# Attention's probabilities turned in one VectorE instruction per unit, the values product in 32x64 tiles, and PSUM cut into three pairs of banks and two single ones

## The chip, the cores and the metric

The kernel runs on one core of a Trainium2 chip. The metric is the device time of one execution in microseconds (us). Before the change it is 827.86 us, the median of three runs (825.67 to 829.38). The engines are named as in the profile: PE is TensorE's matmul, PEld its weight load, DVE is VectorE, ACT is ScalarE, POOL is GpSimd, SP is SyncE, which issues every DMA of this kernel.

## The reference

Attention with two kinds of windows, and two MLPs on its output, all in float32:

```
q, k, v: [4 batches, 8 heads, 576 positions, 64]
scores = q @ k.T / 8
allowed: rel = query - key;  heads 0 to 3: 0 <= rel < 32
                             heads 4 to 7: 0 <= rel < 128 and rel % 4 == 0
attn = exp(scores - max);  attn = attn / (sum(attn) + 1e-9);  out = attn @ v
x = out as [2304 tokens, 512]
x = g(x @ w_in) @ w_out,    g(h) = h / (1 + exp(-1.702 h)),   512 -> 2048 -> 512
x = r(x @ w_in2) @ w_out2,  r(h) = max(h, 0)**2,              512 -> 2048 -> 512
```

## The kernel before, in words

**Attention.** The positions of heads 4 to 7 are reordered by their remainder modulo 4, so that both kinds of heads have a window of 32. The work is cut into 32 *units*: four batches, four pairs of heads (`p`; the two heads of a pair, `j`, lie on the two halves of the partitions) and two halves of the positions (`u`). A unit has 288 queries in three blocks of 96, and each block sees 128 keys. A unit (`attend`) runs through these steps: two loads by SP (`qk`, L476, and `v`, L480); scores on PE (L514); per head and block a maximum with the mask added on DVE (L530) and an exponential with its sum on ACT (L538); `guard` and `recip` (L552, L555) and the division (`normalise`, L562); the turning of the probabilities so that keys lie on partitions; the values product on PE (L616); and two copies into `x`, a rounded high part (L271 on ACT or L273 on DVE) and the rest (L632 on DVE).

There are two ways to score and to turn. In batch 0 (`turn_pe`) a block of 96 queries is scored against its 128 keys by one matmul per head, with masks of 96x128, and turned by PE against an identity (L597), with a copy of the result out of PSUM for each head (`evac`, 128x288). In batches 1 to 3 only the band is computed: per block three groups of 32 queries against their 64 keys, 18 small matmuls in tiles of 64 rows by 32 columns, and the turning takes six DVE instructions of 32x192 (L582) into a tile `pt` that is zero elsewhere. In both the values product is six matmuls of 128 rows by 64 columns, 96 moving columns each.

**Layer 1.** The 2304 tokens are worked in five blocks of 512, 512, 256, 512 and 512 (`BLOCKS1`). In a block, 16 steps (`step`, index `f`) each take 12 matmuls into a bank `h` (L664 to L666), a tanh on ACT (L688), a product on DVE (L691), a split into `gh` and `gl`, and 12 matmuls into four banks `o` (L716 to L718). Every product in full precision is three matmuls of rounded parts, high times high, high times low, low times high. The weights of layer 1 are loaded (`raw`, L332), reassembled by `raw_top` (`c`, L271) and `raw_join` (L343), and split into `wp` high and low while block 0 runs. Batch 0's units come ahead of block 0; the other 24 units are strewn between the matmuls of blocks 0 to 2, eight to each.

**Layer 2** uses seven products for eight, in three pieces of 768 tokens, with weights streamed in from DRAM where blocks 3 and 4 had stored them.

**What sets the order.** All of it is written down as tasks with an engine (or a choice of ACT, DVE, POOL), a cost, a wanted time and buffers. `Schedule.run` takes them one by one in the order of their modelled starts, and emits each engine's instructions in that order. The costs, the wanted times and the margins at the head of the file decide the order, and the chip keeps it. In gaps of PE that the model foresees ahead of layer 1 it emits matmuls on zeros (L775).

**PSUM** has eight banks. Before, four are `o` (layer 1's outputs; early on also scores and values of batch 0), two are `h`, two are `s` (scores, and the values of batches 1 to 3).

Of the kernel before, what the change touches and what calls it, by code (L numbers as in the profile page):

```python
# [37 lines left out]
T_START = 29.61  # L38
T_ATT = 2.78
A0 = 0.27  # L40
A1 = 0.99
BAND_FROM = 1

AHEAD = (32, 35, 48)
# [6 lines left out]
PREP = 9.48  # L51
# [3 lines left out]
RAW_FROM = 3.07  # L55
WARM = 256
MASK_AT = -9.0
LEAD = (12.09, 8.0, 5.51)
SPACE = 3.94
# [3 lines left out]
SPARE_POOL = (3.96, 1.14, 0.0)  # L63
SPARE_ACT = (0.0, 0.07, 0.01)
SPARE_TO = (7.79, 224.45)
# [26 lines left out]
X_EARLY = 18.11  # L92
X_FROM = 2.03
X_WANT = 6.23


class Schedule:
# [3 lines left out]
    def __init__(self, places):  # L101
        self.sizes = places
        self.tasks = []
        self.idle = None

    def buffer(self, cls):
        return {"cls": cls, "users": 0}

    def task(self, engine, cost, want, fn, after=(), bufs=(), port=False, since=0.0, late=0.0):
# [4 lines left out]
            "since": since, "late": late, "n": len(self.tasks), "next": [], "before": 0, "worse": 0.0,  # L114
# [11 lines left out]

    def open(self, t):
        for e, cost in t["ways"].items():
            ready = max([end + (self.SAME[e] if d == e else self.HOP[d] + MORE_HOP) for end, d in t["ready"]] + [t["since"]])
            self.opened[e].append((t, ready, cost, t["worse"] if e == "dve" else 0.0))  # L130

    def run(self, emit):

        engines = self.SAME
        places = {c: [(0.0, None)] * n for c, n in self.sizes.items()}
# [11 lines left out]
        for _ in range(len(self.tasks)):  # L147
# [34 lines left out]
            for b in t["bufs"]:  # L182
                if not b["held"]:
                    b["held"] = True
                    by = places[b["cls"]].pop(0)[1]
# [7 lines left out]
            t["engine"], t["start"] = e, start  # L193
            self.order.append(t)
            if e == "dma":
                issued = max(start, issued) + 0.45
# [7 lines left out]
            for b in t["bufs"]:  # L204
# [3 lines left out]
                if b["left"] == 0:  # L208
                    c = places[b["cls"]]
                    c.append((b["end"] + self.HOP[e], b["by"]))  # L210
                    c.sort(key=lambda p: p[0])
# [9 lines left out]
def attention_mlp_mlp(  # L221
# [18 lines left out]
    psum = {  # L240
        "o": ctx.enter_context(tc.tile_pool(name="ps_o", bufs=4, space=PSUM)),
        "h": ctx.enter_context(tc.tile_pool(name="ps_h", bufs=2, space=PSUM)),
        "s": ctx.enter_context(tc.tile_pool(name="ps_s", bufs=2, space=PSUM)),
    }
# [8 lines left out]
    ident = att.tile([QB, QB], F32, name="ident")  # L253
    mask_sb = att.tile([QB, 5, P], BF16, name="mask_sb")
    mask_band = att.tile([QB, 5, 2 * WIN], BF16, name="mask_band")
    pt = att.tile([P, 2, NBLK, QB], F32, name="pt")

    places = {
        "o": 4, "h": 2, "s": 2, "c": C_BUFS, "qk": 2, "v": 2, "sm": 2, "st": 3, "pt": 1,
# [4 lines left out]
    sched = Schedule(places)  # L264
    task, buffer = sched.task, sched.buffer
# [31 lines left out]
    def bank(cls, name):  # L297
        return psum[cls].tile([P, 512], F32, tag=cls, name=name)
# [105 lines left out]
    def x_pieces(b, p, u):  # L404

        plain = p < NPAIR // 2
        m = HALF // 4
        jobs = []
        for n, blk in enumerate(BLOCKS1):
            size = sum(e - a for _, _, a, e in blk)  # L410
            found = []
            col = 0
            for bb, r, a, e in blk:
                if bb == b:
                    if plain:
                        lo, hi = max(a, m * u), min(e, m * (u + 1))
                        if lo < hi:
                            found.append((r, lo, hi, col + lo - a))
                    elif r // 2 == u:
                        found.append(((r % 2) * ROW + a, (r % 2) * ROW + e, col))  # L420
                col += e - a
            if plain:
                while found:
                    r, lo, hi, c = found.pop(0)
                    rows = 1
                    while (
                        found
                        and found[0] == (r + rows, lo, hi, c + rows * ROW)
                        and c >= lo % ROW
                        and c - lo % ROW + (rows + 1) * ROW <= size  # L430
                    ):
                        found.pop(0)
                        rows += 1

                    def src(o, r=r, rows=rows, lo=lo, hi=hi):
                        v = o[:, 0:HALF].rearrange("p (i r) -> p r i", r=4)
                        v = v[:, r:r + rows, lo - m * u:hi - m * u]
                        return v if rows > 1 else v[:, 0]

                    def dst(x, z, c=c, rows=rows, lo=lo, hi=hi):  # L440
                        if rows == 1:
                            return x[:, z, p, c:c + hi - lo]
                        c0 = c - lo % ROW
                        v = x[:, z, p, c0:c0 + rows * ROW].rearrange("p (r i) -> p r i", r=rows)
                        return v[:, :, lo:hi]

                    jobs.append((n, rows * (hi - lo), src, dst))
            elif found:
                s0, c0 = found[0][0], found[0][2]
                w = sum(f[1] - f[0] for f in found)  # L450
                jobs.append(
                    (
                        n, w, lambda o, s0=s0, w=w: o[:, s0:s0 + w],
                        lambda x, z, c0=c0, w=w: x[:, z, p, c0:c0 + w],
                    )
                )
        return jobs

    MAXIMA, EXPS = {P: 0.205, 2 * WIN: 0.145}, {P: 0.385, 2 * WIN: 0.34}
# [948 lines left out]
```

## Time and profile before

| what | value |
|---|---|
| median of three runs | 827.86 us (825.67 to 829.38) |
| the profiled execution | 826.51 us, span 824.5 us |
| granted TensorE clock, mean | 0.998 |
| stretch 0 to 40 us: PE, DVE, ACT, POOL busy | 30.66, 29.70, 31.65, 18.02 us |
| stretch 40 to 150 us: PE, DVE, ACT busy | 109.83, 97.27, 78.99 us |
| stretch 150 to 300 us: PE, DVE, ACT busy | 150.00, 104.59, 71.87 us |
| stretch 300 to 460 us: PE, DVE, ACT busy | 160.00, 128.14, 78.80 us |
| stretch 460 to 821 us: PE, DVE, ACT busy | 361.00, 235.75, 169.80 us |

The span runs from the first to the last instruction; the execution's own time is 2.0 us longer. The first stretch is batch 0's attention, the second most of block 0 (with the weights' preparation), the third blocks 1 and 2, the fourth blocks 3 and 4, the last layer 2. A matmul's busy time is counted to its modelled end and neighbours overlap, so that 100% of PE says that it never stood empty, not that every matmul ran at its peak.

### The profile page before, as it was taken

How to read it: one execution, taken by the hardware profiler on the slowest of the kernel's cores; microseconds unless marked ns; L12 is line 12 of the kernel's file. 1: busy time of each engine (PE TensorE's matmuls, PEld its weight loads, DVE VectorE, ACT ScalarE, POOL GpSimd, SP SyncE). 2: the span in 40 equal slices, each digit the busy share in tenths (PEclk: the TensorE clock that was granted, in tenths of full speed). 3: DMA queues.
4: the chain of work that ended last, by engine and by line, in shares of the span. 5: the costliest groups of instructions: out<-in, count | busy, mean ns of one | idle time of the engine just before them, and what ended most of it. 6: DMA issues, size and time to landing. Idle time of an engine off the chain costs nothing.

```text
span 824.5 us, 14514 instructions
## 1 busy us (share of the span) xinstructions
PE 811.7 (98%) x5412; PEld 729.6 (88%) x5412; DVE 596.0 (72%) x1467; ACT 431.1 (52%) x1061; POOL 18.6 (2%) x28
## 2 busy tenths in 40 slices
PE   7899999999999999999999999999999999999998
PEld 5687777877789988888888899999999999999998
DVE  6898997755568886878697745589545689365784
ACT  6976775544545563445455345435355446355432
POOL 4400000000000000000000000000000000000000
PEclk9999999999999999999999999999999999999999
DMA  7645564211132129988976761697877686767751
GB/s 238 231 150 212 183 207 155 66 50 34 43 101 73 55 87 297 295 290 304 339 265 241 282 239 49 258 331 257 305 276 258 240 342 236 268 249 269 276 208 57
DMA packets 54917, 171.43 MB, mean 208 GB/s; under 512 B 4736, under 2 KB 26944, under 8 KB 49472
## 3 DMA queue, kind: packets, MB, share of 16 engines
q1 hardware_dynamic: 54848, 170.52, 58.8%
q8 instruction: 42, 0.69, 0.3%
q14 instruction: 27, 0.22, 0.1%
HBM read 131.70 MB, written 38.80 MB: 207 GB/s over the span
## 4 chain that ended last, share of the span: by engine, by line
PE 96%; DMA 2%; ACT 1%; DVE 1%; SPq 0%; issue 0%; DVEq 0%
PE o L716 9%; PE h L664 8%; PE o L718 8%; PE o L717 8%; PE h L665 8%; PE h L666 8%; PE X L1097 4%; PE X L1096 4%; PE X L1095 4%; PE X L1252 3%; PE X L1250 3%; PE X L1251 3%; PE pv L616 2%; PE Y L1252 2%; PE Z L1097 2%; PE Y L1250 2%
## 5 line engine op out<-in xcount | busy, mean ns | idle before, releaser
L664 PE MATMUL h<-x,wp 128*128 128x512 f32 (+3 forms) x328 | 122.1, 372 | 0.2 <-DVE g L691 0.2
L716 PE MATMUL o<-gh,wp 128*128 128x512 f32 (+3 forms) x328 | 122.2, 372 | 0.0
L665 PE MATMUL h<-x,wp 128*128 128x512 f32 (+3 forms) x328 | 119.5, 364 | 0.4 <-DVE x L632 0.3
L666 PE MATMUL h<-x,wp 128*128 128x512 f32 (+3 forms) x328 | 119.3, 364 | 0.0
L717 PE MATMUL o<-gh,wp 128*128 128x512 f32 (+3 forms) x328 | 119.3, 364 | 0.0
L718 PE MATMUL o<-gl,wp 128*128 128x512 f32 (+3 forms) x328 | 119.3, 364 | 0.0
L271 ACT CAST gh<-gq 128x768 fp32r<-128x768 f32 x84 | 68.9, 837 | 74.4 <-PE X L1251 20.9
L282 DVE TENSOR_TENSOR gl<-gq,gh 128x768 fp32r<-128x768 f32 x84 | 80.4, 957 | 28.1 <-PE X L1252 12.2
L688 ACT ACTIVATE g<-h 128x512 f32<-128x512 f32 (+3 forms) x82 | 44.6, 545 | 82.7 <-PE h L666 82.6
L716 PEld LDWEIGHTS o<-gh,wp 128*128 128x128 f32 x328 | 61.7, 188 | 12.0
L664 PEld LDWEIGHTS h<-x,wp 128*128 128x128 f32 x328 | 61.8, 188 | 11.9 <-DVE g L691 0.3
L691 DVE SCALAR_TENSOR_TENSOR g<-g,h 128x512 f32<-128x512 f32 (+3 forms) x82 | 50.8, 620 | 29.2 <-ACT g L688 28.3
L718 PEld LDWEIGHTS o<-gl,wp 128*128 128x128 f32 x328 | 61.8, 188 | 10.0
L665 PEld LDWEIGHTS h<-x,wp 128*128 128x128 f32 x328 | 61.8, 188 | 10.0 <-DVE x L632 0.8
L666 PEld LDWEIGHTS h<-x,wp 128*128 128x128 f32 x328 | 61.8, 188 | 10.0
L717 PEld LDWEIGHTS o<-gh,wp 128*128 128x128 f32 x328 | 61.8, 189 | 9.5
L538 ACT ACTIVATE sm<-sm,st 96x64 f32<-96x64 f32 (+1 forms) x180 | 62.4, 349 | 13.8 <-DVE st L530 13.6
L582 DVE STREAM_TRANSPOSE pt<-sm 32x192 f32<-32x192 f32 x144 | 53.1, 368 | 5.8 <-ACT sm L277 3.8
L282 DVE TENSOR_TENSOR gl<-g,gh 128x512 fp32r<-128x512 f32 (+3 forms) x82 | 51.0, 622 | 7.3 <-ACT gh L271 6.1
L1117 DVE TENSOR_TENSOR gq<-u,Z 128x384 f32<-128x384 f32 x48 | 26.6, 554 | 40.6 <-ACT u L271 23.8
L271 ACT CAST gh<-g 128x512 fp32r<-128x512 f32 (+3 forms) x56 | 33.7, 601 | 37.2 <-DVE g L691 18.6
L271 ACT CAST c<-raw 128x512 f16<-128x512 bf16 x52 | 40.5, 779 | 22.6 <-DMA raw<-in_w 21.5
(131 smaller groups left out, 1796.5 us busy)
## 6 DMA issues: line engine op xcount, KB each, us to landing
ws<-wo_s SPq DMA_DIRECT2D x42, 1024.0 KB, 7.1
raw<-in_w SPq DMA_DIRECT2D x64, 511.8 KB, 4.9
ws<-wi_s SPq DMA_DIRECT2D x36, 896.0 KB, 6.4
wo_s<-wt SPq DMA_DIRECT2D x16, 896.0 KB, 6.9
wi_s<-wt SPq DMA_DIRECT2D x16, 896.0 KB, 6.5
qk<-in_qkv SPq DMA_DIRECT2D x32, 304.0 KB, 2.9
v<-in_qkv SPq DMA_DIRECT2D x32, 192.0 KB, 2.3
xs<-x2d SPq DMA_DIRECT2D x12, 384.0 KB, 4.8
```

The source lines that it names most:

```text
L271: A.copy(out, in_)
L282: by_name[e].tensor_tensor(out=out, in0=a, in1=b, op=ALU.subtract)
L538: A.activation(out=m["sm", j][:, i], in_=m["sm", j][:, i], func=AF.Exp, bias=m["st"][:, 0, j, i:i + 1], scale=-1.0, accum_out=m["st"][:, 1 ...
L582: V.transpose(out=pt[32 * e:32 * e + 32, :, :, 32 * a:32 * a + 32].rearrange("p j i q -> p (j i) q"), in_=m["sm"][32 * a:32 * a + 32, :, : ...
L664: T.matmul(out, w_hi[:, ks], x[:, 0, k, a:z], start=(k == 0), stop=False)
L665: T.matmul(out, w_hi[:, ks], x[:, 1, k, a:z], start=False, stop=False)
L666: T.matmul(out, w_lo[:, ks], x[:, 0, k, a:z], start=False, stop=(k == KD - 1))
L691: V.scalar_tensor_tensor(out=g(), in0=g(), scalar=1.0, in1=h(), op0=ALU.add, op1=ALU.mult)
L716: T.matmul(out, w_hi[:, ds_], m["gh"], start=(f == 0 and a == 0), stop=False)
L717: T.matmul(out, w_lo[:, ds_], m["gh"], start=False, stop=False)
L718: T.matmul(out, w_hi[:, ds_], m["gl"], start=False, stop=(f == KF - 1))
L1097: T.matmul(out, wt[:, 1, a, ks], hi, start=False, stop=(k == 1), skip_group_check=True)
```

## The change

1. **All four batches score the band.** The masks of 96x128 are no longer used, the identity and the turning on PE with its copies out of PSUM are gone, and ACT and DVE work on 64 keys for a query in batch 0 too. The masks come by four smaller DMAs.
2. **One turning per unit.** DVE transposes the unit's whole 96x384 in one instruction (32x32 squares), where it had six of 32x192 in batches 1 to 3.
3. **The values product in 32x64 tiles.** Without the zeros in `pt`, the product of a group of 32 queries is the sum over two groups of 32 keys: 36 matmuls of 32 rows by 64 columns, 32 moving columns each, in place of six. Which queries lie where is rearranged: partition group `a` now holds a whole block of 96, and each row group writes a bank of its own (`ab[0]`, `ab[1]`, `c`). `v` is loaded to 96 partitions, as four segments of 512 bytes each, by three DMAs per unit.
4. **The copies into `x`** take the result from two banks at once and from the third by itself, so a unit's copies come in more pieces.
5. **PSUM** is one tile of eight banks: three pairs (`pr`) and two single banks (`h`). A unit's scores take a pair; its values take a pair and one `h`, the class that layer 1's hidden products use. Layer 1's outputs take two pairs. Once attention and block 4's first steps are through, the pairs fall apart into `o` (four banks) and `s` (two), as before.
6. **The numbers** that the planner works with are others; a line of them is in the diff.

```diff
-RAW_FROM = 3.07
+RAW_FROM = 7.67
...
-    "o": ctx.enter_context(tc.tile_pool(name="ps_o", bufs=4, space=PSUM)),
-    "h": ctx.enter_context(tc.tile_pool(name="ps_h", bufs=2, space=PSUM)),
-    "s": ctx.enter_context(tc.tile_pool(name="ps_s", bufs=2, space=PSUM)),
+    psum = ctx.enter_context(tc.tile_pool(name="psum", bufs=1, space=PSUM)).tile([P, 8, 512], F32, name="ps")
...
+    sched.parts["pr"] = {0: [("o", 0), ("o", 1)], 1: [("o", 2), ("o", 3)], 2: [("s", 0), ("s", 1)]}
...
+        qk_b, v_b, sm_b, st_b, pt_b, s_b, ab_b, c_b = (buffer(c) for c in ("qk", "v", "sm", "st", "pt", "pr", "pr", "h"))
...
-            m["v"] = qkv.tile([P, UV], F32, tag="v", bufs=2, name="v")
-            nc.sync.dma_start(m["v"], src[:, UQ + UK:])
+            m["v"] = qkv.tile([QB, NBLK + 1, P], F32, tag="v", bufs=2, name="v")
+            for a in range(NBLK):
+                at = UQ + UK + a * P
+                nc.sync.dma_start(
+                    m["v"][a * WIN:(a + 1) * WIN], src[:, at:at + P].rearrange("(t k) d -> k t d", t=NBLK + 1)
+                )
...
-        def band(a, e):
-            V.transpose(
-                out=pt[32 * e:32 * e + 32, :, :, 32 * a:32 * a + 32].rearrange("p j i q -> p (j i) q"),
-                in_=m["sm"][32 * a:32 * a + 32, :, :, 32 * (e - a):32 * (e - a) + 32].rearrange("p j i q -> p (j i) q"),
-            )
...
-                    for i in range(NBLK):
-                        T.transpose(m["t", j][:, i * QB:(i + 1) * QB], m["sm", j][:, i], ident)
-                def evac(e, j=j):
-                    copy(e, flat(pt[:, j]), m["t", j][:, 0:NBLK * QB])
...
+        def turn():
+            m["pt"] = att.tile([QB, 2, NBLK, 2, WIN], F32, tag="pt", bufs=2, name="pt")
+            V.transpose(out=m["pt"].rearrange("k j i e q -> k (j i e q)"), in_=m["sm"].rearrange("q j i c -> q (j i c)"))
...
         def values():
-            m["o"] = bank(pv_cls, "pv")
+            m["ab"], m["c"] = bank_pair(ab_b), bank(c_b)
             for i in range(NBLK):
-                for j in range(2):
-                    js = slice(D * j, D * (j + 1))
-                    T.matmul(
-                        m["o"][js, i * QB:(i + 1) * QB], m["v"][:, i * P + D * j:i * P + D * (j + 1)],
-                        pt[:, j, i], start=True, stop=True,
-                    )
+                for e in range(2):
+                    for a in range(NBLK):
+                        rows = slice(a * WIN, (a + 1) * WIN)
+                        for j in range(2):
+                            js = slice(D * j, D * (j + 1))
+                            o = m["ab"][js, a] if a < 2 else m["c"][js]
+                            T.matmul(
+                                o[:, i * WIN:(i + 1) * WIN], m["v"][rows, i + e, js], m["pt"][rows, j, i, e],
+                                start=(e == 0), stop=(e == 1), tile_position=(a * WIN, D * j), skip_group_check=True,
+                            )
...
-        h_cls = "s" if f % 2 and late else "h"
+        h_cls = "pr" if f % 2 and late and f < KF - 2 else "h"
...
-            blk["o_buf"] = [buffer("o") for _ in range(KD)]
+            blk["o_buf"] = [b for b in (buffer("pr"), buffer("pr")) for _ in range(2)]
```

How the order changes is shown at three places. First ACT's instructions at the program's start, before: `sm` and `g` hold scores of batch 0, `c` and `wp` are weights, `tp` is the turned result in PSUM, `x` is layer 1's input.

```order
L538 ACTIVATE sm,st<-sm,st 96x128 x12
L271 CAST wp<-raw 128x512
L271 CAST c<-raw 128x512
L271 CAST wp<-raw 128x512
L538 ACTIVATE g,st<-g,st 96x128 x2
L271 COPY pt<-tp 128x288
L538 ACTIVATE g,st<-g,st 96x128 x4
L271 CAST x_294<-pv 128x3x72
```

And now (`ps` is all of PSUM):

```order
L537 ACTIVATE sm,st<-sm,st 96x64 x15
L284 CAST x_311<-ps 128x3x48
L284 CAST x_311<-ps 128x3x24
L284 CAST x_311<-ps 128x24
L537 ACTIVATE sm,st<-sm,st 96x64 x3
L284 CAST c<-raw 128x512
L537 ACTIVATE sm,st<-sm,st 96x64
```

Ahead of the first tanh of layer 1 ACT has 48 exponentials in both. Its nine copies out of PSUM are gone, its two casts `c` fewer are made later, and its casts into `x` are 22 where there were 9.

Next SP's queue of DMAs at the start, before:

```order
L748 DMA mask_sb<-in_masks 96x256
L749 DMA mask_sb<-in_masks 96x384
L476 DMA qk<-in_qkv 128x608 x2
L480 DMA v<-in_qkv 128x384 x2
L332 DMA raw<-in_w 128x2047 x3
L476 DMA qk<-in_qkv 128x608 x4
L480 DMA v<-in_qkv 128x384
L332 DMA raw<-in_w 128x2047
L476 DMA qk<-in_qkv 128x608
L332 DMA raw<-in_w 128x2047
```

And now:

```order
L728 DMA mask_sb<-in_masks 96x128
L729 DMA mask_sb<-in_masks 96x128
L497 DMA qk<-in_qkv 128x608
L732 DMA mask_sb<-in_masks 96x256
L733 DMA mask_sb<-in_masks 32x64
L497 DMA qk<-in_qkv 128x608
L503 DMA v<-in_qkv 32x4x128 x6
L497 DMA qk<-in_qkv 128x608 x2
L350 DMA raw<-in_w 128x2047 x3
L497 DMA qk<-in_qkv 128x608
```

The three weights now stand behind the fourth `qk`, where they stood behind the second; the next weight comes after ten `qk`, where it came after six.

Last PE in block 1, around a values product, before:

```order
L666 MATMUL h<-x_337,wp 128x512
L616 MATMUL pv<-pt,v 64x96 [waits DMAHW2_49,DVE_49,PE_49]
L616 MATMUL pv<-pt,v 64x96 x5
L664 MATMUL h<-x_337,wp 128x512
L665 MATMUL h<-x_337,wp 128x512
```

And now:

```order
L696 MATMUL ps<-gl,wp 128x512 [waits DVE_49]
L589 MATMUL ps<-pt,v 64x32 [waits DMAHW0_49,DVE_49]
L589 MATMUL ps<-pt,v 64x32
L589 MATMUL ps<-pt,v 64x32 [waits DMAHW1_49]
L589 MATMUL ps<-pt,v 64x32
L589 MATMUL ps<-pt,v 64x32 [waits DMAHW2_49,DVE_49]
L589 MATMUL ps<-pt,v 64x32 x31
L694 MATMUL ps<-gh,wp 128x512
```

The product waits for three loads in place of one. It stood inside a group of hidden products (`h`); it now stands at their boundary, since it takes one of the two banks `h`, and behind it come output products.

## Rows read from the trace of the kernel before

**Rows 1.** The page's head: span, then busy us and share of each engine.

```profile
span 824.5 us, 14514 instructions
...
PE 811.7 (98%) x5412; PEld 729.6 (88%) x5412; DVE 596.0 (72%) x1467; ACT 431.1 (52%) x1061; POOL 18.6 (2%) x28
```

**Rows 2.** Chain that ended last, 0 to 42 us: start, us, what held it.

```profile
18.39 0.74 SPq L332
...
19.70 6.27 DMA qk<-in_qkv
...
40.65 0.13 PE o L716
```

**Rows 3.** One stage: length; busy us of PE, PEld, DVE, ACT, POOL; clock, DMA.

```profile
6.59:37.20 30.61, 24.66 (x282) 18.92 (x280) 26.47 (x154) 27.56 (x121) 13.60 (x15) 0.94 0.71 243
```

**Rows 4.** Timeline of ACT: start us, us, what (several merged in a row).

```profile
29.76 0.52 ACT L271 CAST x<-pv 128x216 fp32r<-128x216 f32 x3
...
32.01 0.39 ACT L538 ACTIVATE sm<-sm,st 96x128 f32<-96x128 f32 x1
...
32.39 0.39 ACT L538 ACTIVATE sm<-sm,st 96x128 f32<-96x128 f32 x1
...
35.14 0.38 ACT L271 CAST x<-pv 128x288 fp32r<-128x288 f32 x1
...
35.42 0.39 ACT L271 COPY pt<-tp 128x288 f32<-128x288 f32 x1
...
35.71 0.77 ACT L271 CAST c<-raw 128x512 f16<-128x512 bf16 x1
...
36.35 0.38 ACT L271 COPY pt<-tp 128x288 f32<-128x288 f32 x1
...
37.50 0.35 ACT L538 ACTIVATE sm<-sm,st 96x64 f32<-96x64 f32 x1
...
37.83 0.35 ACT L538 ACTIVATE sm<-sm,st 96x64 f32<-96x64 f32 x1
```

**Rows 5.** DVE groups by line and shape: count | busy us, mean ns.

```profile
L582 DVE STREAM_TRANSPOSE pt<-sm 32x192 f32<-32x192 f32 x144 | 53.1, 368 | 5.8 <-ACT sm L277 3.8
...
L530 DVE CUSTOM_DVE_ANT_0 sm<-s,mask_band 96x64 f32<-96x64 f32 x144 | 22.7, 215 | 1.8 <-PE s L514 1.4
...
L530 DVE CUSTOM_DVE_ANT_0 sm<-s,mask_sb 96x128 f32<-96x128 f32 x36 | 8.1, 281 | 8.3 <-PE s L514 5.3 <-PE tp L597 2.8 <-POOL g L562 0.3
```

**Rows 6.** Timeline of PE in block 2, around scores and a values product.

```profile
263.34 0.28 PE L718 MATMUL o<-gl,wp 128*128 128x256 f32 x1
...
263.55 0.62 PE L514 MATMUL s<-qk 64*32 64x64 f32 x36
...
264.32 0.28 PE L717 MATMUL o<-gh,wp 128*128 128x256 f32 x1
...
265.51 0.28 PE L666 MATMUL h<-x,wp 128*128 128x256 f32 x1
...
265.72 0.72 PE L616 MATMUL pv<-pt,v 128*64 128x96 f32 x12
...
266.59 0.28 PE L665 MATMUL h<-x,wp 128*128 128x256 f32 x1
```

**Rows 7.** Short stages, scores alone: PE, PEld busy; in brackets, records in flight.

```profile
263.62:263.67 0.04, 0.04 (x12) 0.04 (x18) 1.00 0.00 0
263.67:263.68 0.01, 0.01 (x12) 0.01 (x15) 1.00 0.00 0
263.68:263.72 0.04, 0.04 (x18) 0.04 (x18) 1.00 0.00 0
```

**Rows 8.** Scores, values, 40 to 300 us: weight loads, ns min/median/max.

```profile
L514 PEld LDWEIGHTS s<-qk x792: 102/107/107, 68.8 to 294.2; 64*32 64x32 f32 x198
...
L616 PEld LDWEIGHTS pv<-pt,v x288: 132/137/137, 41.0 to 296.4; 128*64 128x64 f32 x144
```

**Rows 9.** Timeline of DVE: the last copies of a unit into x.

```profile
267.10 0.58 DVE L632 TENSOR_TENSOR x<-pv,x 128x64 fp32r<-128x64 f32 x3
```

More of the change, by code (lines that the diff above doesn't have):

```diff
@@ L102, in __init__ @@
         self.sizes = places
+        self.parts = {}
         self.tasks = []
@@ L106, in buffer, with task @@
     def buffer(self, cls):
-        return {"cls": cls, "users": 0}
-    def task(self, engine, cost, want, fn, after=(), bufs=(), port=False, since=0.0, late=0.0):
+        return {"cls": cls, "users": 0, "id": None}
+    def task(self, engine, cost, want, fn, after=(), bufs=(), port=False, since=0.0, late=0.0, count=1):
         many = isinstance(engine, tuple)
@@ L113, in task @@
             "ways": ways, "many": many, "want": want, "fn": fn, "bufs": bufs, "port": port,
-            "since": since, "late": late, "n": len(self.tasks), "next": [], "before": 0, "worse": 0.0,
+            "since": since, "late": late, "count": count, "n": len(self.tasks), "next": [], "before": 0, "worse": 0.0,
         }
@@ L134, in run, with give @@
         engines = self.SAME
-        places = {c: [(0.0, None)] * n for c, n in self.sizes.items()}
+        places = {c: [(0.0, None, i) for i in range(n)] for c, n in self.sizes.items()}
+        apart = False
+        def give(c, end, by, i):
+            for d, k in self.parts[c][i] if apart and c in self.parts else [(c, i)]:
+                places[d].append((end, by, k))
+                places[d].sort(key=lambda p: p[0])
         self.opened = {e: [] for e in engines}
@@ L193, in run @@
             t["engine"], t["start"] = e, start
+            if t["fn"] == self.fall_apart:
+                apart = True
+                for c in self.parts:
+                    rest, places[c] = places[c], []
+                    for end, by, i in rest:
+                        give(c, end, by, i)
             self.order.append(t)
             if e == "dma":
-                issued = max(start, issued) + 0.45
+                issued = max(start, issued) + 0.45 * t["count"]
                 moved = max(issued + 0.65, moved) + cost
@@ L622, in attend @@
+        pv = task("pe", VALUES, want, values, [moved, d_v], [pt_b, v_b, ab_b, c_b])
         att_tasks.append(pv)
@@ L668, in step @@
             before = [t] if t else [chain["hidden"]] if "hidden" in chain else []
+            if f < 2 and k == 0:
+                before = before + [v for u in range(2) if z > FIRST or u == 0 for v in values_of[blk["i"], u]]
             t = task(
```

333 lines of the change are left out of this document (155 added, 178 removed).

## The prediction

> **What bounds the kernel now.** I read the head of the page first. PE is busy for 811.7 us of a span of 824.5 [rows 1], and the reader is to see there that no other engine is near that, so that from the first dense matmul on the time is what PE has queued. Only two things can then move the end: what PE itself has to do, and how long it takes until its queue is dense. For the second I read the chain over the first 42 us: it goes through loads, ACT and DVE, and PE's dense run begins with the first output product of layer 1 at 40.65 [rows 2]. Next the stage from ACT's first exponential at 6.59 to its first tanh at 37.20: of 30.61 us ACT is busy for 27.56, DVE for 26.47, PE for 24.66 (much of that matmuls on zeros), and the DMA engines moved 243 GB/s, busy for 0.71 of it [rows 3]. So ACT sets the start, with DVE close behind and the loads third. The timeline of ACT gives the price of one piece there [rows 4], the groups of DVE theirs [rows 5], and the timeline of PE in block 2, where it never stands empty, what a unit costs in the dense part [rows 6]. The profiled execution took 826.51 us, 2.0 more than its span and 1.4 under the median of 827.86; the sum is made against 826.5.
>
> **The start: ACT.** The 48 exponentials of batch 0 stand ahead of the first tanh in both orders. One on 128 keys takes 0.38 from start to start (32.01 to 32.39), one on 64 keys 0.33 (37.50 to 37.83) [rows 4]: 48 x 0.05 = 2.4 less. The nine copies out of PSUM that go took 0.29 each (35.42 to 35.71) [rows 4]: 2.6 less. Two casts `c` at 0.64 (35.71 to 36.35) [rows 4] move behind the tanh: 1.3 less. Against that, 22 casts into `x` where there were 9. Three casts for one unit took 0.52 where one took 0.38 [rows 4], 0.07 for each further piece, so 13 x 0.07 = 0.9 more; and 504 columns that DVE had cast come to ACT, at 0.28 for 288 (35.14 to 35.42) [rows 4] some 0.4 more, estimated. ACT: -2.4 - 2.6 - 1.3 + 0.9 + 0.4 = -5.0 us.
>
> **The start: DVE.** It must shrink as much, or it takes ACT's place. The maxima fall by 281 - 215 = 66 ns each [rows 5], 48 of them: 3.2. Five copies out of PSUM go, 1.5 at ACT's price. Two joins, three weight parts and one cast fewer stand ahead of the first tanh, some 3 us, estimated at 0.5 apiece beside ACT's 0.64 for a cast `c`. Seven new turnings come in. The trace has none of 96x384; one of 32x192 took 368 ns [rows 5], twice the columns can't be more than 0.74, and the whole cannot be under 0.37: I take 0.55, 3.9 more. Twelve more copies into `x` at ACT's 0.07: 0.8 more. DVE: about -3, on 26.47 us. It was 1.1 us less busy than ACT, and after this it stands at 23.5 against ACT's 22.5. So DVE would let the start gain about 4, ACT 5. Both engines also had idle time in the stage (4.1 and 3.1 us), part of which is the `qk` load that took 6.27 us from its issue at 19.70, behind a weight that SP could issue only at 18.39 when its buffer came free [rows 2]. In the new order no weight stands between the fifth and the tenth `qk`, so that wait has no cause in the same place; I keep it all the same, since `v` now asks for three issues per unit on that queue. I take -4.5. Ends: -7.5 with that wait gone, -1.5 if the loads take over (below).
>
> **Values in the dense part.** Take the distance from the last matmul before a group to the second one after it, with neighbours of one size. Around the 36 records of a unit's scores it is 264.32 - 263.34 = 0.98, around the 12 of its values 266.59 - 265.51 = 1.08 [rows 6]. (A float32 matmul leaves two records.) The new values are 72 records of 32 columns in six tiles; the scores are 36 of 64 in six tiles. Three things could set them:
> - columns: as many in all as the scores have, so 0.98, 0.10 less than now;
> - the rate at which records begin: in flight are 12, still 12, then 18 within the next 0.04 us [rows 7], so six begin in 0.04, and 72 take 0.48, where the 36 took 0.62 - 0.22 = 0.40 from first to last [rows 6] (a record lasts about 0.22): 0.98 + 0.08 = 1.06, 0.02 less than now;
> - weight loads: one of 32 columns takes 107 ns, one of 64 takes 137 [rows 8], which I read as 30 ns per 32 columns; a tile that needs 60 ns of loading for each record has 12 rounds of 0.06 = 0.72: 0.98 + 0.32 = 1.30, 0.22 more than now.
>
> I take the second, since rows 7 show that rate and none shows a faster one. Times 24 units: -0.5 us, from -2.4 to +5.3. Batch 0's eight products lie beside ACT's work.
>
> The Trainium skill has a rule that speaks against small matmuls: its page TensorE: Matmul & The Clock Gate, section "Wait — 56ns, not 53.3ns?", says that matmuls never start closer than about 25 ns, however few their columns. Six records in 0.04 us, in different tiles, are closer than that, so the trace does not bear it out here.
>
> **What costs nothing, and its cover.** In blocks 0 to 2 DVE loses five turnings per unit and gains copies into `x`; PE is busy without a gap there (the table of stages above), so I count nothing. `c` takes one of the two hidden banks until the last copy into `x`, which began at 267.10 and took 0.58 with its like, about 1.2 us after the values [rows 6, 9]. PE has output products of at least that length queued behind the values, so I count nothing; if half of that showed in each of the 24 units, it would be +14. `v` in three loads costs SP two more issues per unit, during which SP has nothing urgent in blocks 0 to 2. Layer 2 has the same products and the same banks.
>
> Sum: 826.5 - 4.5 - 0.5 = 821.5 us.
>
> **Rivals.**
> - *Weight loads set the values.* The third bound: 826.5 - 4.5 + 5.3 = 827.3, no change. For it: the tile loads twice the columns for half the stream [rows 8]. Against: in the scores six tiles loaded side by side and nothing there measures how a tile's next load lies beside its stream.
> - *The loads set the start.* At 243 GB/s and a share of 0.71 [rows 3] there is a third of DMA time left, and short segments of `v` may eat it; then the start gains 1.5: 824.5, at the edge of no change. For it: both long waits of the chain are `qk`. Against: fewer weights stand ahead.
> - *Row tiles run one after another.* If only the two column tiles of a row group overlap, as today, the 72 records are 36 rounds: a third of today's six rounds of (0.72 - 0.25) / 6 = 0.08 each makes 0.026, so 0.94 for 0.47, +0.47 per unit, +11 in all; with 0.06 of loading each, 2.2, +40 in all: 833 to 862, slower. It decides from +0.23 per unit on, where the start's gain is used up and 0.5% lost only from +0.42 on. Against it: the scores mix two row groups with three column groups and begin six at a time [rows 7].
> - *The hidden bank is missed.* The +14 above less the start's 5: 835.5, slower, if ACT and DVE come late to the copies.
> - *A matmul in 25 ns.* By the rule above, made to hold for each of the 36 matmuls: 0.90 from first to last where the scores took 0.40, 1.48 for 1.08, +9.6: 831.6. The rule is the one of the Trainium skill just cited; rows 7 speak against it.
>
> **How the numbers follow.** The forecast 0.52; weight loads 0.19; loads at the start 0.13; row tiles 0.05; the hidden bank 0.07; the 25 ns 0.04. The median's distance from the profile adds up to 1.4 either way. About 0.5% (4.1 us, so 823.7 and 832.0) is what a measurement can tell from no change. Faster: 0.48 of the forecast, whose own range is 817 to 824, 0.05 of the second and 0.04 of the third: 0.57. Slower: row tiles, the hidden bank and a part of the rest: 0.13. Same: 0.30. The range for 8 in 10 is 815 to 830: below, the `qk` wait gone and columns setting the values (826.5 - 7.5 - 2.4 = 816.6, less 1.4); above, weight loads with the median's distance.
>
> **What would show it.** The first output product of layer 1 near 36 in place of 40.65; ACT's stage to its first tanh some 5 us shorter, DVE's turnings of 96x384 between 0.4 and 0.74; the distance around a values product in block 2 near 1.06 (0.98, 1.30 and 1.5 tell the others); PE without a gap in front of hidden products in blocks 0 to 2. Wrong would be a start that does not move, or PE waiting for DVE ahead of hidden products.

## The result, and the profile after

The changed kernel takes 835.47 us (835.13 to 837.95), the kernel before 826.76 in the same series: 1.0109 times as long, 95% interval 1.0073 to 1.0145. It is slower by 1.1%; 821.5 was forecast. The profiled executions took 835.73 and 826.51 us.

The page's head answers to [rows 1]; PEclk is the granted clock in 40 slices:

```profile
span 834.0 us, 18713 instructions
...
PE 821.1 (98%) x7480; PEld 739.8 (89%) x7480; DVE 570.9 (68%) x1443; ACT 411.8 (49%) x1052; POOL 10.7 (1%) x23
...
PEclk9799999999999999999999999999999999999999
```

PE has 2068 more matmul records than before and is busy 9.4 us longer, in the same share of the span; DVE, ACT and POOL got lighter. Where the 9.5 us of span lie is read from layer 1's output products: the first began at 40.49 us before and 44.42 after, the last at 471.31 and 480.61. So the start lost 3.9, the dense part of layer 1, from its first to its last output product (430.8 to 436.2), 5.4, and layer 2 nothing.

**The dense part.** The timeline of PE around one values product in block 2, as in [rows 6]:

```profile
263.55 0.28 PE L641 MATMUL ps<-x,wp 128*128 128x256 f32 x1
263.76 0.98 PE L589 MATMUL ps<-pt,v 32*64 32x32 f32 x72
264.66 0.39 PE L694 MATMUL ps<-gh,wp 128*128 128x256 f32 x1
264.89 0.28 PE L695 MATMUL ps<-gh,wp 128*128 128x256 f32 x1
```

The distance is 264.89 - 263.55 = 1.34, where it was 1.08. Less the two neighbours' own spacing (0.12 each at 256 columns, 0.23 at 512) I call it the *place* of the product: 0.84 before, and now 1.10 to 1.12. 24 x 0.26 would be 6.2 us. But in the order before, the values of batch 0's eighth unit came only behind the first output product, so its dense part held 25 values products: 24 x 1.10 - 25 x 0.84 = 5.4, which is all of this part's loss. The eighth unit's 0.84 is a part of what the start lost.

**The start.** The stage from ACT's first exponential to its first tanh, as [rows 3], then the two stretches of one clock level each that lie around the first hidden products:

```profile
6.06:38.24 32.18, 26.20 (x771) 19.97 (x777) 19.69 (x155) 22.43 (x123) 7.55 (x10) 0.92 0.64 179
29.75:33.16 3.41, 2.00 (x146) 1.68 (x139) 2.29 (x14) 2.88 (x11) 1.76 (x2) 1.00 0.43 120
33.16:43.40 10.24, 10.04 (x196) 9.18 (x196) 5.84 (x31) 5.69 (x31) 0.83 (x1) 0.50 0.78 225
```

ACT's work fell from 27.56 to 22.43 and DVE's from 26.47 to 19.69, and yet the stage is 1.6 longer: PE is the busiest now. The matmuls on zeros alone, in the same stage before and now (PE's busy time is the first number behind the comma):

```profile
6.59:37.20 30.61, 6.51 (x31) 3.62 (x31) 0.94 0.71 243
6.06:38.24 32.18, 8.13 (x33) 3.98 (x33) 0.92 0.64 179
```

Without them PE had 24.66 - 6.51 = 18.2 us of work before, with the clock at 2.4 GHz from 9.93 to 27.0, and has 26.20 - 8.13 = 18.1 now, at 1.2 GHz up to 29.75: it did not get lighter in time where ACT and DVE did. Of the 3.9 us, 1.0 is lost up to the first tanh (37.20 and 38.24) and 2.9 between it and the first output product. There PE now runs a unit's scores, two units' values and 12 hidden products, these at 0.24 us each.

That the clock was at 1.2 GHz before 29.75 is read from the matmuls: those on zeros, of 256 columns, came 0.21 apart (the profile's 1.00 ahead of the first rise says nothing). From the chain that ended last over the first 46 us (start, us, what; L517 scores, L589 values, L770 zeros, L639 to L641 hidden products, L694 output product):

```profile
8.23 1.82 PE ps L770 x8
...
13.63 2.73 issue
16.36 0.45 PE ps L517 x10
...
23.67 1.40 PE ps L770 x6
25.06 1.52 PE ps L589 x72
26.59 0.90 PE ps L517 x36
...
28.43 2.21 ACT sm L537 x13
...
32.05 1.32 issue
...
38.20 1.45 PE ps L589 x72
...
44.49 0.33 PE ps L694
```

Where [rows 2] went through loads, ACT and DVE, this chain runs mostly through PE: values at 1.5 us a unit and scores at 0.9, zeros between them, and twice "issue", a stop in the middle of a product with nothing to wait for that the profile shows. Two stretches of it, 19.3 to 21.3 and 27.5 to 31.3, still run through ACT and DVE.

### The profile page after: what moved, and what is told of

It reads as the page before. It is cut to its first block, busy times and chain, and to the rows that moved or that the text cites. A ratio compares the mean times of both kernels' runs of the same rounds, so it can differ in the third digit from the quotient of the medians.

```text
span 834.0 us, 18713 instructions
## 1 busy us (share of the span) xinstructions
PE 821.1 (98%) x7480; PEld 739.8 (89%) x7480; DVE 570.9 (68%) x1443; ACT 411.8 (49%) x1052; POOL 10.7 (1%) x23
## 4 chain that ended last, share of the span: by engine, by line
PE 98%; issue 1%; DMA 1%; DVE 0%; ACT 0%; SPq 0%
PE ps L639 9%; PE ps L694 9%; PE ps L640 8%; PE ps L641 8%; PE ps L695 8%; PE ps L696 8%; PE ps L1244 7%; PE ps L1088 7%; PE ps L1089 7%; PE ps L1243 7%; PE ps L1245 7%; PE ps L1090 7%; PE ps L589 4%; PE ps L517 2%; PE ps L770 1%
## 5 line engine op out<-in xcount | busy, mean ns | idle before, releaser
L639 PE MATMUL ps<-x,wp 128*128 128x512 f32 (+3 forms) x328 | 123.1, 375 | 0.0
L694 PE MATMUL ps<-gh,wp 128*128 128x512 f32 (+3 forms) x328 | 122.2, 373 | 0.0
L640 PE MATMUL ps<-x,wp 128*128 128x512 f32 (+3 forms) x328 | 120.5, 367 | 0.0
L641 PE MATMUL ps<-x,wp 128*128 128x512 f32 (+3 forms) x328 | 120.4, 367 | 0.0
L695 PE MATMUL ps<-gh,wp 128*128 128x512 f32 (+3 forms) x328 | 119.3, 364 | 0.0
L696 PE MATMUL ps<-gl,wp 128*128 128x512 f32 (+3 forms) x328 | 119.3, 364 | 0.0
L1245 PE MATMUL ps<-gl,ws 128*128 128x384 f32 x336 | 112.2, 334 | 0.0
L1243 PE MATMUL ps<-gh,ws 128*128 128x384 f32 x336 | 112.2, 334 | 0.0
L1244 PE MATMUL ps<-gh,ws 128*128 128x384 f32 x336 | 112.2, 334 | 0.0
L1088 PE MATMUL ps<-xo,ws 128*128 128x384 f32 x252 | 84.2, 334 | 0.0
L1089 PE MATMUL ps<-xo,ws 128*128 128x384 f32 x252 | 84.2, 334 | 0.0
L1090 PE MATMUL ps<-xo,ws 128*128 128x384 f32 x252 | 84.2, 334 | 0.0
L537 ACT ACTIVATE sm<-sm,st 96x64 f32<-96x64 f32 x192 | 64.5, 341 | 22.7 <-DVE st L530 22.4
L639 PEld LDWEIGHTS ps<-x,wp 128*128 128x128 f32 x328 | 62.8, 192 | 11.0 <-ACT sm L537 0.2
L641 PEld LDWEIGHTS ps<-x,wp 128*128 128x128 f32 x328 | 62.9, 192 | 10.0
L694 PEld LDWEIGHTS ps<-gh,wp 128*128 128x128 f32 x328 | 61.7, 188 | 11.1
L640 PEld LDWEIGHTS ps<-x,wp 128*128 128x128 f32 x328 | 63.0, 192 | 9.0
L696 PEld LDWEIGHTS ps<-gl,wp 128*128 128x128 f32 x328 | 61.8, 188 | 10.1
```

Of the source, the lines that this page charges most:

```text
L639: T.matmul(out, w_hi[:, ks], x[:, 0, k, a:z], start=(k == 0), stop=False)
L640: T.matmul(out, w_hi[:, ks], x[:, 1, k, a:z], start=False, stop=False)
L641: T.matmul(out, w_lo[:, ks], x[:, 0, k, a:z], start=False, stop=(k == KD - 1))
L694: T.matmul(out, w_hi[:, ds_], m["gh"], start=(f == 0 and a == 0), stop=False)
L695: T.matmul(out, w_lo[:, ds_], m["gh"], start=False, stop=False)
L696: T.matmul(out, w_hi[:, ds_], m["gl"], start=False, stop=(f == KF - 1))
```

## The experiments

All are edits of the changed kernel, except beforenw; `before` was timed beside each. "First" is where layer 1's first output product begins; it and the place are read from one profiled execution of each. The changed kernel was timed in four executions, and the intervals of warm, warm8, rawlate and afternw overlap widely with its own (that of v24dense at its edge): where these differ from it by some us, the times alone don't show it.

| run | median us | ratio to before (95%) | first | place of values |
|---|---|---|---|---|
| changed kernel | 835.47 | 1.0109 (1.0073 to 1.0145) | 44.42 | 1.10 |
| v24b | 825.88 | 0.9990 (0.9973 to 1.0007) | 38.62 | 0.92 |
| v24 | 826.22 | 0.9984 (0.9972 to 0.9997) | 36.61 | 0.92 |
| v24start | 829.75 | 1.0036 (1.0022 to 1.0050) | 38.55 | 1.10 |
| v24dense | 832.54 | 1.0065 (1.0047 to 1.0083) | 44.74 | 0.92 |
| olddense | 844.74 | 1.0208 (1.0188 to 1.0228) | 45.53 | 0.85 |
| warm | 834.36 | 1.0084 (1.0063 to 1.0104) | 42.74 | 1.11 |
| v24warm | 827.80 | 1.0008 (0.9995 to 1.0021) | 38.98 | 0.93 |
| warm8 | 838.64 | 1.0136 (1.0115 to 1.0158) | 45.18 | 1.10 |
| v24bw8 | 832.39 | 1.0052 (1.0034 to 1.0071) | 42.62 | 0.92 |
| rawlate | 839.61 | 1.0141 (1.0120 to 1.0162) | 49.45 | 1.11 |
| stA | 829.01 | 1.0020 (1.0006 to 1.0033) | 39.34 | 0.92 |
| stB | 837.65 | 1.0122 (1.0100 to 1.0143) | 44.88 | 0.92 |
| beforenw | 827.88 | 1.0012 (0.9996 to 1.0028) | 42.60 | 0.84 |
| afternw | 833.47 | 1.0083 (1.0065 to 1.0101) | 40.71 | 1.10 |
| v24bnw | 826.58 | 0.9983 (0.9967 to 0.9998) | 38.28 | 0.92 |
| stAnw | 827.44 | 1.0007 (0.9995 to 1.0018) | 37.87 | 0.92 |

### Fewer matmuls for the same values

The keys of group `t` of 32 belong to two neighbouring groups of queries, whose turned probabilities lie side by side in `pt`. So one load of `v[t]` can serve both.

```diff
-            for i in range(NBLK):
-                for e in range(2):
+            for t in (1, 3, 0, 2):
...
-  o[:, i * WIN:(i + 1) * WIN], m["v"][rows, i + e, js], m["pt"][rows, j, i, e],
-  start=(e == 0), stop=(e == 1),
+  o[:, cols], m["v"][rows, t, js], p_[:, lo * WIN:hi * WIN],
+  start=(t % 2 == 1),     # v24;   v24b: start=(t == 1)
```

v24:

> The changed kernel, but a unit's values product in 24 matmuls instead of 36: the block of v that is the second half of one window's keys and the first half of the next one's is loaded once and streams 64 columns, so 48 records in place of 72, in 8 rounds of six tiles in place of 12. Theory A (a tile takes its next record only when its load and its stream are through; 96 columns took 58 ns a round): 2 x (71 + 58 + 58 + 71) = 516 ns from first to last for 758, so the place of a values product falls from 1.10 us to about 0.87, 24 x 0.23 = 5.5 us in the dense part, with a little at the start: 829, between 826 and 831. Theory B (the 9 us come from elsewhere: the hidden bank given to c, the order, copies that come late): the place of the values may shrink, but the time stays within 833 to 836.

v24b:

> As v24 (24 matmuls for a unit's values), but only the first matmul into a bank carries the start mark; in v24 two did, and the sums that the first had written were lost. Same instructions, same order, same columns. Theory A (rounds of six tiles): the place of a values product is again 0.92 us, the dense part of layer 1 (first to last output product) 4 to 5 us shorter than the changed kernel's 436.2, and the time 826, between 824 and 828, as v24. If the mark itself cost time, another place than 0.92.

Two `start` marks in a bank cost v24 what its first matmuls had written (the same holds for v24warm below). The Trainium skill (PSUM — Partial Sum Buffer, "The four PSUM rules") says that the mark acts on the whole bank in the partitions written, and this fits. The time is the same with one mark: 9.6 us under the changed kernel, level with before. Around a product of v24b:

```profile
254.72 0.28 PE L643 MATMUL ps<-x,wp 128*128 128x256 f32 x1
254.93 0.80 PE L591 MATMUL ps<-pt,v 32*64 32x64 f32 x48
255.65 0.39 PE L696 MATMUL ps<-gh,wp 128*128 128x256 f32 x1
255.88 0.28 PE L697 MATMUL ps<-gh,wp 128*128 128x256 f32 x1
```

The place is 1.16 - 0.24 = 0.92, not 0.87. The half that theory A did not price is the start: its first output product comes 5.8 us earlier. v24start and v24dense (the same edit under `if start` and `if not start`) part the two:

> The changed kernel with the 24-matmul values product in batch 0 only; batches 1 to 3 keep 36. Theory A+S (the loss has two parts: PE's part of the start, where each record counts because PE is what the chain runs through there at 1.2 GHz; and 0.18 us per unit in the dense part): of the 9.6 us that v24b gained, the start's 5 to 6 come, the dense part's 4.4 do not: 830, between 828.5 and 831.5; first output product between 37 and 40 and not 44.42; place of a values product in the dense part 1.10. If the start does not depend on the values' records, 835 and 44.

> The other half: 24-matmul values products in batches 1 to 3, 36 in batch 0. Theory A+S: first output product at 43 to 45 as in the change, place of a values product 0.92, 24 x 0.18 = 4.4 us less in the dense part: 831, between 829.5 and 832. With v24start it should add up to v24b's gain of 9.6 within 1.5 us.

Batch 0's eight units give 5.7 us, the other 24 give 2.9 (4.4 expected); the sum of 8.6 is 1.0 short of v24b's 9.6. What the 24 lack fits the clock: in v24dense's profiled execution it fell once more, inside the dense part.

```profile
45.57:48.99 3.42, 3.42 (x18) 3.42 (x17) 2.38 (x9) 2.04 (x9) 0.00 (x0) 0.50 0.42 74
```

3.42 us at half the clock hold 1.7 us of PE's work, and this dense part is 1.5 longer than v24b's (433.4 and 431.9). So the values' records are what both losses hang on, and a unit counts four to six times as much in the start (0.71 us against 0.12 to 0.18). From the start of v24start's chain:

```profile
14.15 1.79 issue
...
22.39 1.19 PE ps L592 x48
```

A product is 0.3 to 0.4 us shorter there, some 2.8 for the eight; the rest goes with shorter stops (1.79 in the chain for 4.05), and loads stand in the chain in their place. How much of the 5.7 is PE's own time and how much fewer instructions is not separated.

### The old form in the dense part

Batches 1 to 3 turn by six instructions and multiply in 12 records again:

```diff
+        if old:
+            moved = [task("dve", 0.38, want, lambda a=a, e=e: band(a, e), ...)
+                     for a in range(NBLK) for e in (a, a + 1)]
```

> The changed kernel, but the units of batches 1 to 3 have the form of before: six turnings by VectorE each, values in 12 matmuls of 128 rows. Batch 0, the eight banks of PSUM and the planner's numbers stay those of the change. Theory A (the values' form costs 1.10 us of PE per unit in the dense part where the old one cost 0.84): 835.5 - 24 x 0.26 = 829.2, between 828 and 831, with the first output product at 44.4 as in the changed kernel. Theory B (the hidden bank, the order or the copies cost it): the bank of c is still a hidden one here, so the time stays at 833 to 837.

A miss in its total: the place fell to 0.85 as theory A says, but the kernel got 9 us slower, 8 of them behind layer 1's last output product. Its waits (engine, line, for whom: us, times, longest), one from 46 to 150 us, two at the border of the layers:

```profile
PE ps L525 <- DVE x L638: 3.5, 3, 1.4
```

```profile
ACT ost L292 <- DMA x2d<-ost: 6.0, 1, 6.0
PE ps L1124 <- ACT ost L292: 5.9, 1, 5.9
```

With six turnings DVE comes late to the copies that free the pairs of banks, and layer 2 waits for a store. That the order, made for the new form, is the reason is not shown. This undo moves too much to price the values by time; what it shows is the place.

### What sets the place

narrow halves the columns of each load, and so leaves out half of the values; rowwise puts the loop over `a` outermost, so that one row group's two tiles are in turn at a time.

```diff
-  js = slice(D * j, D * (j + 1))          # narrow
+  js = slice(D * j, D * j + D // 2)
...
-            for i in range(NBLK):               # rowwise
-                for e in range(2):
-                    for a in range(NBLK):
+            for a in range(NBLK):
+                for i in range(NBLK):
+                    for e in range(2):
```

> The changed kernel, but each of the 36 matmuls of a values product loads 32 columns of v and not 64, so half of the values (d 32 to 63 of each head) are left out. Records, order and streamed columns are the same. Theory L (weight loads set it: 30 ns per 32 columns, 12 rounds): the place of a values product falls from 1.10 to about 0.74. Theory R (the price is by the record, 36 in 0.40 us in the scores and 72 in 0.76 here, whatever their columns): it stays between 1.05 and 1.12. A round of six is 58 ns now; L 28 to 30, R 55 to 58.

> The changed kernel, but the 36 matmuls of a values product go row group by row group (12 of the first, 12 of the second, 12 of the third) and not by turns, so that two tiles stand side by side in place of six. Theory R1 (a tile takes its next record some 55 to 58 ns after the last one, and tiles run beside each other): 36 rounds of 56 ns, 2.0 us from first to last, place 2.3 us, 24 x 1.2 = 30 us more: 862 to 870. Theory R2 (PE starts a record every 9.6 to 12 ns, whichever tile): 1.10 as now, 835.

One execution each: 832.01 and 864.25 us beside 828.15 for before. One values product of narrow, then one of rowwise (its neighbours have 512 columns):

```profile
255.01 0.82 PE L589 MATMUL ps<-pt,v 32*32 32x32 f32 x72
```

```profile
240.41 0.39 PE L641 MATMUL ps<-x,wp 128*128 128x512 f32 x1
240.72 1.89 PE L589 MATMUL ps<-pt,v 32*64 32x32 f32 x72
242.54 0.50 PE L694 MATMUL ps<-gh,wp 128*128 128x512 f32 x1
242.88 0.40 PE L695 MATMUL ps<-gh,wp 128*128 128x512 f32 x1
```

Narrow's place is 0.95: neither L's 0.74 nor R's 1.10. The loads' width is worth 0.155 us of the 0.26; that the rest is the number of records fits v24b (a third fewer, 0.18 less) but was not changed by itself. Rowwise's is 2.47 - 0.46 = 2.01 (R1 said 2.3): in it pairs of records start 58 ns apart, so a tile that loads 64 columns takes its next record after 58 ns, and only other tiles fill that time. Six tiles make 58 ns a round in the changed kernel's first 36 records; the second half of its product is slower, 0.43 us for 36. With 32 columns loaded the first 32 records begin within 0.20 us, 6.4 ns apart, and the later ones slow down as well. What slows the second half of a long product stays open.

### The clock, or PE's queue

`warm` adds bursts of matmuls on zeros, `warm8` lets the planner's own go on to the end of batch 0 (and into another bank), and v24warm and v24bw8 do so on top of v24 and v24b.

```diff
+            if start:                                   # warm: after scores 3, after values 5
+                burst(m["s"][:, 0, 256:480], 3)
...
-        task("pe", 0.0, T_START, warm_end, att_tasks[:WARM_FOR], [warm_b, zeros_b])
+        task("pe", 0.0, T_START, warm_end, list(att_tasks))   # warm8
```

> The changed kernel, with matmuls on zeros added in batch 0 (8 ahead of the first scores, 3 after each scores product, 5 after each values product, 224 columns each). In the changed kernel the granted clock of TensorE was the lower level until 29.75 us and again from 33.16 to 43.40. Theory C (the start is late because PE does its part of it at 1.2 GHz): the clock rises before 12 us and stays, scores take 0.41 us from first to last and not 0.57, values 0.76 and not 1.23, the first output product comes at 40 or earlier in place of 44.42: 831, between 828 and 832. Theory D (the start is set by gaps in PE's instruction supply, 2.73 us at 13.63 and 1.32 at 32.05, or by the loads): the clock rises, but the first output product comes no earlier than 43 and the time stays at 834 to 837, as the added matmuls are more instructions.

> Both edits at once. Theories A and C: the savings add, 835.5 - 5.5 - 4.5 = 825.5, between 822 and 828. If only the values matter (A without C) 829, if only the clock (C without A) 831, if neither 834 to 837.

> The changed kernel; matmuls on zeros go into PE's planned idle time until the end of batch 0 (in the changed kernel they end with its fifth values product), and they write into unused columns of another bank, so that both hidden banks are free. Theory C (the start is late because the clock falls at 33.16 and stays at 1.2 GHz until 43.40): the clock is at 2.4 GHz while batch 0's last units and the first hidden products run (24 x 0.107 = 2.6 us of those, 0.3 to 0.5 per unit), the first output product comes 3 to 5 us earlier than 44.42: 831, between 829.5 and 832.5. Theory D (instruction supply and loads set the start): it comes no more than 1 us earlier, 834 to 836.

> v24b and warm8 together. v24's clock rose at 25.31 and never fell, without these matmuls. So C expects little beyond v24b: 825, between 823 and 827. If the added instructions make PE's gaps longer (D), 827 to 829.

None of the four bears theory C out. In `warm` the clock was at 2.4 GHz from 11.62 to 18.45 and from 25.28 on, and a values product took 0.97 us for 1.5; yet the start gained only 1.7 us. But the bursts stood in the chain themselves (0.6 us behind each values product, 0.3 to 0.7 behind the scores, 6.4 us in all), and so did a `qk` load of 7.83 us. So what the clock alone would give stays open: no run gives PE the higher clock and nothing more to do. In `warm8` the matmuls on zeros did not bring the clock up before 39.94; it took 3 us more, 0.8 of them at the start and 1.8 behind layer 1, where its order had moved too with the hidden bank that it frees. v24b without and with them: 825.88 and 832.39, 4.0 of it at the start. v24warm lies in the range that A and C together gave, but v24 without the bursts lies lower (826.22), so it does not speak for C.

Then the other way round, the matmuls on zeros taken out and the order left alone:

```diff
     def keep_warm():
-        T.matmul(warm["o"][:, 0:WARM], warm["zeros"][:, 0:P], warm["zeros"], start=True, stop=True)
+        pass
```

> The kernel before, without the matmuls on zeros that fill PE's idle time in batch 0; all else in its order. Theory C (clock): the clock, at 2.4 GHz from 9.93 to 27.0 in before, stays at 1.2 for most of the start; the first output product comes 1 to 3 us after 40.49: 829, between 828 and 831. Rival (ACT and DVE set before's start and PE has time to spare, at either clock): first output product within 0.7 us of 40.49, 826.5 to 827.5.

> The changed kernel without the matmuls on zeros. They did not raise the clock before 29.75 there, and lay in the chain for 10% of the first 46 us. Theory P (PE's own queue at 1.2 GHz sets the start): 1 to 3 us of them come off, the clock is the lower one throughout: first output product 42 to 44, 833.5 (832 to 835). Theory C: without them the clock rises later still, and it gets 1 to 2 us slower: 836 to 838.

> v24b without the matmuls on zeros. In v24b they lay in the chain for 7.7% of its first 42 us, but the clock was at 2.4 GHz from 28.5 to 35.4. Theory P: within 1 us of v24b either way, 825 to 827; theory C: first output product 2 us later, 828.

Before neither gains nor loses by them in time (1.0012), though its profiled start came 2.1 later, as C said. The changed kernel took 2.0 us less without them, as theory P said, in intervals that overlap. In the profiles its first output product came 3.7 earlier, which is more than P gave and level with before, with the clock at 1.2 GHz until 36.41. So no gain by the zeros shows here. Two rows of its chain and two of PE's waits to 45 us:

```profile
27.84 1.51 PE ps L589 x72
...
34.14 0.24 PE ps L641
```

```profile
PE ps L517 <- DMA qk<-in_qkv: 8.3, 4, 4.7
PE ps L589 <- DVE pt L575: 2.8, 3, 1.4
```

At the low clock still (288 columns in 0.24), but PE now waits for loads and turnings instead of being behind. In v24b, whose units take PE some 0.35 less each in the start, they make no difference (825.88 and 826.58).

### The gaps, and the weights

rawlate moves the first weight loads; stA and stB are v24b with those loads spread between the `qk` loads, stAnw is stA without zeros.

```diff
-RAW_FROM = 7.67
+RAW_FROM = 16.0                                              # rawlate
-        ... load, (), [raw_b], since=RAW_FROM)
+        ... since=RAW_FROM if want - LEAD[0] < 5 else max(RAW_FROM, min(want - LEAD[0], 13) + 4.0))  # stA
```

> The changed kernel, but the planner may not load weights before its time 16 (7.67 in the change). In the changed kernel three weight loads of 512 KB went out at 8.73 to 10.1, the DMA engines were busy for 0.99 of 10 to 15 us, PE's next 16 KB of instructions began to move only at 13.99, and PE stood from 13.63 to 16.36. Theory D (instructions wait behind data): the gap of 2.73 us shrinks under 1.2 and the first output product comes 1.5 to 3 us earlier: 833, between 831.5 and 834. Theory C alone: the gap may go, but the half clock keeps the first output product at 43 to 45: 835 to 836.

> v24b, with the three first weight loads (512 KB each, issued together at 8.71 ahead of the fourth qk load, which took 6.95 us there and stood in the chain from 10.94 to 17.93) set apart: one stays where it is, the others go behind the fifth and the sixth qk load. Theory Q (the rest of the start is that qk load behind weights): the load of the fourth qk falls to 4 us or less, the first output product from 38.6 to 36 or earlier, 823.5 (822 to 825.5). Rival: the later weights hold up the first hidden products, or the instructions do, and it stays at 825 to 828.

> As stA, but the first of the three weight loads too goes behind the fourth qk load. Theory Q: the fourth qk lands in 3 us; 823 (821.5 to 825). Rival: the first weights are split too late and the first hidden product, at 30.3 in v24b, comes after 32: 826 to 830.

> stA without the matmuls on zeros. In stA the qk wait is gone, but PE at 1.2 GHz (1.19 + 0.88 us per unit and the zeros' matmuls between) is what its chain runs through from 20 to 39 us. Theory P: without the zeros' matmuls the units close up, first output product at 36.5 to 38 where stA has 39.3: 826.5 (825 to 828). Theory C: no earlier than stA, 829 to 831.

From rawlate's chain:

```profile
12.74 0.78 PE ps L517 x26
13.53 0.45 PE ps L517 x10
...
21.61 7.14 DMA qk<-in_qkv
```

The product that had stopped for 2.73 us runs through. The stretch of 10 to 15 us, first in the changed kernel, then in rawlate (columns as [rows 3]; the DMA engines' share is the last but one):

```profile
10.00:15.00 5.00, 3.63 (x137) 2.74 (x136) 2.87 (x21) 3.86 (x20) 1.38 (x2) 1.00 0.99 379
```

```profile
10.00:15.00 5.00, 4.99 (x159) 3.40 (x162) 3.41 (x29) 3.39 (x21) 1.24 (x2) 1.00 0.49 138
```

The transfer that brings PE's next 16 KB of instructions began at 13.99 in the changed kernel, after the stop had begun at 13.63, and at 10.90 in rawlate. So that gap was most likely instructions behind data; the later stops were not tested this way. But the weights, now at 18.6, held up a later `qk` for 7.14 us, and the first output product came at 49.45, so that rawlate missed the ranges of both theories. In v24b the same wait stands elsewhere in the chain:

```profile
10.94 6.95 DMA qk<-in_qkv
...
33.24 1.18 issue
```

stA removed it and gained nothing at the start (39.34); it took 3.1 us more than v24b, which lie behind its first output product, in an order that the edit had moved. With PE's zeros out too it came to 37.87 and 827.44, which can't be told from v24b. Theory Q fell: one wait goes and PE is late next. stB lies outside both of its ranges. Its `qk` wait did not go, it moved (7.71 us from 15.13). Its first hidden product came at 38.0, where its rival had said after 32, and at the border of the layers PE waits for a store as in olddense:

```profile
PE ps L1090 <- ACT ost L290: 5.9, 1, 5.9
```

## Why the prediction was wrong

- **The start, ACT and DVE: the bound was wrong.** ACT's work in the stage fell by 5.1 (5.0 forecast), DVE's by 6.8 (3, so under by half, on the side that should have helped). A turning took 570 ns (550):

```profile
L575 DVE STREAM_TRANSPOSE pt<-sm 96x384 f32<-96x384 f32 x32 | 18.2, 570 | 3.3 <-ACT sm L290 2.0 <-POOL sm L562 1.0
```

  The step that failed is "So ACT sets the start", with the sentence that batch 0's eight products "lie beside ACT's work". [rows 3] had PE at 24.66 of 30.61. I set that aside as matmuls on zeros, but these were only 6.51 of it, and the change takes nothing off the other 18: the eight units alone are now 8 x (1.52 + 0.90) = 19.4 us at 1.2 GHz, with zeros in order between the products and two stops of 4.05 together. So once ACT and DVE were lighter, PE's queue was next. v24start (5.7 us by fewer records) and afternw (first output product 3.7 earlier by no zeros) show that queue as the bound, with ACT's, DVE's and SP's instructions as they were. -4.5 became +3.9. How the 3.9 divides between the clock, the stops and the new order of the hidden products is not shown; the planner's numbers, which changed along, were not tried by themselves.
- **The values: the wrong row for the rate.** I took 6.7 ns a record from six that begin in 0.04 us [rows 7] and left out the pause up to the next six. [rows 6] had it: 36 records in 0.40 us, 11 ns each, so about 0.8 for 72; measured 0.76. The distance is 1.34, the rival *weight loads set the values* had 1.30 and is nearest, though narrow gives the loads only 0.155 of the 0.26. -0.5 became +5.4 (with one unit fewer in the dense part).
- **Row tiles one after another:** no. Rowwise shows the price if they did, 29 us. The limits of this rival, +0.23 and +0.42 per unit, don't come out of its own sums (4.5 / 24 = 0.19 and 8.6 / 24 = 0.36); nothing hangs on them.
- **A matmul in 25 ns** (Trainium skill, TensorE: Matmul & The Clock Gate, "Wait — 56ns, not 53.3ns?"): 72 records in 0.76 us are 10.5 ns each, or 21 for each of the 36 matmuls, and 17 in narrow (0.63 us); no run here bears the rule out for small tiles side by side. Within one tile the starts are 58 ns apart.
- **The hidden bank:** nothing, as counted. From the first output product on PE has no gap of 0.06 us or more in the changed kernel.
- **The loads:** PE's scores waited 3.6 us for `qk` in the changed start. They were not the bound while PE was behind; rawlate shows them become it.
- **Not foreseen:** PE's two stops, 2.73 and 1.32 us, the first most likely for want of instructions.

No version here beats the kernel before by more than can be told: v24b 0.9990 and v24bnw 0.9983. With 24 matmuls the change gains 1.9 us at the start (38.62 for 40.49), and loses 24 x 0.92 - 25 x 0.84 = 1.1 in the dense part (431.9 for 430.8).

## What to carry to other kernels

Work that seems to lie beside the bound must be summed at the clock it will have: when a busy engine gets lighter by 5 us, ask which engine's own total is next, and count its records and its fillers, not its columns. Small matmuls in many tiles are paid by the record and by the columns that each loads, so look for operands that can be shared between neighbours before splitting further. Matmuls on zeros are only free while the engine has time to spare; leave them out once, to see what they are worth: in none of the four kernels without them did the time get longer beyond the noise.

## What the runs showed of the hardware that I had not expected

- A tile that loads 64 columns took its next float32 record after 58 ns, with one or with three row groups in turn; six tiles in turn gave 9.7 ns a record, and with 32 columns loaded 6.4 ns, for the first 32 to 36 records of a product; after that 8 to 12 ns.
- PE stopped in the middle of a product, with no wait that the profile shows, for 0.4 to 4.6 us in nearly every form with 32-row tiles; one of these stops went when weight loads were moved out of the way of PE's instructions. The kernel before had none in its start (beforenw one of 1.0).
- With small tiles and zeros by turns the clock stayed at 1.2 GHz for up to 40 us (warm8), without the zeros for up to 36 (afternw), and in v24b the time did not depend on them.
